# Heads of Q and K in 20 rows each of the DRAM scratch, read back by overlapping loads of 32 rows, one head group a load

## The chip, the cores and the metric

The kernel runs on one core of a Trainium2 chip. A core has TensorE (PE, with its weight loads shown as PEld), VectorE (DVE), ScalarE (ACT), GpSimd (POOL) and SyncE (SP), each with its own stream of instructions, and sixteen DMA engines that carry the transfers which SP and ACT issue. The metric is the device time of one execution in microseconds.

## The reference

The input x has 2048 rows of 640. After a layer norm, two branches are added to x: sliding-window attention with 32 heads of 20 and a window of 256, and a gated MLP with 1536 hidden columns.

```
xn  = layernorm(x)
qkv = xn @ wqkv;  q, k, v: 32 heads x 2048 x 20
p   = softmax(q k^T / sqrt(20)), key j seen by query i when 0 <= i - j < 256
A   = (p v) @ wo
B   = (sigmoid(xn @ w_gate) * (xn @ w_up)) @ w_down
out = x + A + B
```

## The kernel before, in words

The rows go in four chunks of 512 (`CW`). For a chunk, five projection blocks give Q and five give K, each 128 output columns by 512 rows, transposed: output columns on the partitions (`proj_block`, matmuls at L311). DVE copies a Q block to SBUF (L315), ACT a K block (L317), into `st`, of which there are six buffers. SP then stores the block to a DRAM scratch, `sq` or `sk` (L319). The weight columns are picked so that block m holds rows 4m to 4m+3 of every head.

[...] `spread` (L329) loads 128 scratch rows, which are four heads, onto 128 partitions; one load takes two such head groups, 256 KB. There are eight head groups of four heads (`NG` = 8), in two halves of four (`GH`), each half in one `qT` or `kT` tile. The matmul of the scores (L502, in `scores`) reads partitions 32i to 32i+19 of the tile, 20 of the 32.

One pair of scratch tensors serves all chunks, so the stores of the next chunk follow the loads of this one.

Everything that PE does stands in an order written out by hand. `scores` steps (four per pair of head groups in the first chunk, five in the later ones) alternate with pieces of other work that the class `Fill` hands out: gate and up matmuls (`g_gu`, L425 and L432), the next chunk's Q, K and V projections (`g_qk`, `g_v`), and the output products (`g_out`, L446 and L453). PE takes them strictly in that order. ACT takes the exponential of each step's scores (L508), POOL masks it (L519), and `pv` multiplies by V (L535).

The norm of the next chunk is also in there (`g_norms`): DVE normalizes four blocks of rows, SP writes each to a DRAM tile `xs` (L287), reads it back regrouped (L293), and DVE turns it in 32x32 squares into `xnT` (L296), five turns a chunk. The next chunk's projections read `xnT`.

All loads and stores but a few at the very end are issued by SP, in program order. An issue that must wait for a tile, a buffer or an earlier transfer holds back those behind it. Transfers signal on eight semaphores that are used in turn. In SP's queue of the first chunk, the order after the projections is: loads of Q groups 0 and 1, K groups 0 and 1, Q 2 and 3, K 2 and 3; four weight loads of 480 KB (`load_rest`, L180); Q and K groups 4 to 7; the four `xs` writes and four regrouped reads; x rows for chunk 2; eight copies that reorder `wo` in DRAM (`turn_wo`, L207, tile `wo_i`, outermost dimension 4); the loads of `wd`. In a later chunk, the four loads for Q and K of the first half and then the four of the second half follow one another.

Of the kernel before, what the change touches and what calls it, by code (L numbers as in the profile page):

```python
# [9 lines left out]
P = 128  # L10
S = 2048
D = 640
H = 32
DH = 20
# [3 lines left out]
CW = 512  # L18
NCH = S // CW
SBC = CW // P  # L20
HG = 4
NG = H // HG
GH = NG // 2
# [14 lines left out]
BF16 = mybir.dt.bfloat16  # L38
# [55 lines left out]
def kernel(  # L94
# [11 lines left out]
    nc = tc.nc  # L106
# [4 lines left out]
    def pool(name, bufs, **kw):  # L111
        return ctx.enter_context(tc.tile_pool(name=name, bufs=bufs, **kw))

    const = pool("const", 1)
# [5 lines left out]
    kp = pool("kp", 5)  # L120
# [47 lines left out]
    load_wqkv(0)  # L168
    load_wqkv(1)

    scratch = {w: tc.dram_tile([H * 32, CW], BF16, name="s" + w) for w in "qk"}
    zero = kp.tile([P, GH, CW], BF16, name="kT")
    nc.gpsimd.memset(zero[:, 0:3, :], 0.0)

    def clear(w):
        rows = scratch[w].rearrange("(h j) s -> h (j s)", j=32)[:, DH * CW:]
        nc.sync.dma_start(out=rows.rearrange("h (a e) -> h a e", a=4), in_=zero[:, 0:3, :])

    def load_gu(t, w, k, lo=0, hi=FS):
        nc.sync.dma_start(out=t[k][:, :, lo:hi],  # L180
# [2 lines left out]
    load_gu(wg, B_w_gate, 0, 0, FS // 2)  # L183
    load_gu(wu, B_w_up, 0, 0, FS // 2)
    clear("q")
    clear("k")
    load_gu(wg, B_w_gate, 0, FS // 2)

    def load_rest():
        load_gu(wg, B_w_gate, 1, 0, FS // 2)  # L190
        load_gu(wu, B_w_up, 1, 0, FS // 2)
        load_gu(wg, B_w_gate, 1, FS // 2)
        load_gu(wu, B_w_up, 1, FS // 2)
        spread("q", 0, 4, NG)
        spread("k", 0, 4, NG)
# [107 lines left out]
    qk = {}  # L303
    vt = {}

    def proj_block(w, c, m):

        ps = ps_d.tile([P, CW], FP32, name="pqk", tag="d")
        for d in range(DC):
            wt = wqkv["qk".index(w)][:, d, :].rearrange("p (k m) -> p m k", m=DC)  # L310
            nc.tensor.matmul(ps, lhsT=wt[:, m, :], rhs=xnT[c][:, d, :],  # L311
                             start=(d == 0), stop=(d == DC - 1))
        st = stp.tile([P, CW], BF16, name="st")
        if w == "q":
            nc.vector.tensor_copy(out=st, in_=ps)  # L315
        else:
            nc.scalar.copy(out=st, in_=ps)  # L317
        dst = scratch[w].rearrange("(h j) s -> h j s", j=32)
        nc.sync.dma_start(out=dst[:, 4 * m:4 * m + 4, :], in_=st)  # L319

    def spread(w, c, g0, g1):

        half, first = divmod(g0, GH)
        if first == 0:
            qk[w, c, half] = (qp if w == "q" else kp).tile([P, GH, CW], BF16, name=w + "T")
        src = scratch[w].rearrange("(a b p) s -> b p a s", a=2, p=P)
        for b in range(g0 // 2, g1 // 2):
            o = 2 * b - half * GH
            nc.sync.dma_start(out=qk[w, c, half][:, o:o + 2, :], in_=src[b])  # L329

    def new_v(c, s):
        v = vp.tile([P, 2, VH], BF16, name="v")
# [47 lines left out]
    def g_qk(c):  # L380
        for w in "qk":
            for m in range(DC):
                proj_block(w, c, m)
                if c == 0 and w == "q" and m == 1:
                    load_x(1)
                if c == 0 and w == "q" and m == 3:
                    load_gu(wu, B_w_up, 0, FS // 2)
                if c == 1 and w == "q" and m == 3:
                    load_wo()
                if c and w == "k" and m == DC - 1:  # L390
                    spread("q", c, 0, GH)
                yield 5 * MM
        if c == 0:
            spread("q", c, 0, 2)
            spread("k", c, 0, 2)
            spread("q", c, 2, 4)
            spread("k", c, 2, 4)
# [63 lines left out]
    def new_rows(c, s, rows=None, queue=nc.sync):  # L461
        if rows is None:
            rows = lnp.tile([P, D], BF16, name="rows", bufs=3)
        queue.dma_start(out=rows, in_=xr[:, c * SBC + s, :])
        return rows
# [292 lines left out]
    c = NCH - 1  # L758
# [5 lines left out]
    rows = [new_rows(c, s, queue=nc.scalar) for s in range(SBC - 1)]  # L764
# [57 lines left out]
```

## Time and profile before

| | |
|---|---|
| median of three runs | 309.14 us (308.84 to 310.28) |
| the profiled execution | 309.41 us, span 307.7 us, granted PE clock 1.00 |
| PE, ACT, DVE, POOL busy | 98%, 64%, 58%, 55% of the span |
| transfers | 36.87 MB, 120 GB/s over the span |
| SP's issues of Q and K loads | 16 + 16, 256 KB each |
| SP's issues of Q and K stores | 20 + 20, 128 KB each |

The span runs from the first to the last instruction; the profiled execution's own time is 1.71 us longer. An engine's share is its busy time over the span. The page's timeline in 40 slices has 7.7 us to a slice, and its DMA row is the mean busy share of the sixteen DMA engines. In timelines, a line has the start, the duration, the engine, the source line, the operation and its tiles; SPq stands for SP's issuing. An issue's duration is the time in which SP handled it and not that of the transfer. The trace also records when a transfer's parts arrive, one record for each DMA engine that took part.

### The profile page before, as it was taken

What the parts mean: (1) busy time and instruction counts of PE and PEld (TensorE: products, weight loads), DVE (VectorE), ACT (ScalarE), POOL (GpSimd) and SP (SyncE); (2) the same over time, 40 slices, a digit from 0 to 9 for tenths busy, and PEclk for the clock granted to TensorE, in tenths of its full rate; (3) what the DMA queues carried; (4) which work ended last, traced back from release to release, by engine and by line L of the source; (5) the groups of instructions that cost most, each with busy time, mean ns of one, the idle gap of its engine ahead of it and who ended that gap; (6) DMA issues with size and microseconds to landing.
All of it is one profiled execution on the core that took longest, in us unless ns stands there. A gap on an engine that the chain in (4) does not pass through costs nothing.

```text
span 307.7 us, 9969 instructions
## 1 busy us (share of the span) xinstructions
PE 300.1 (98%) x4276; PEld 167.6 (54%) x4311; DVE 178.1 (58%) x355; ACT 198.4 (64%) x197; POOL 168.3 (55%) x307
## 2 busy tenths in 40 slices
PE   7999999999999999999999999999999999999995
PEld 2654444545657654554557664554546664444774
DVE  4735539888675564497946464383734536373423
ACT  5933777698854649888674647878585547678000
POOL 3110687687982928676682728557372937566000
PEclk9999999999999999999999999999999999999999
DMA  7997967886528052800036212730000210000202
GB/s 201 362 336 249 314 201 188 306 244 203 170 92 171 21 179 69 278 33 2 3 131 130 66 58 88 249 123 0 2 2 2 79 34 21 2 2 3 86 21 68
DMA packets 40173, 36.87 MB, mean 120 GB/s; under 512 B 8992, under 2 KB 39840, under 8 KB 40096
## 3 DMA queue, kind: packets, MB, share of 16 engines
q1 hardware_dynamic: 39264, 35.45, 37.7%
q10 hardware_dynamic: 864, 0.77, 0.8%
q8 instruction: 34, 0.56, 0.7%
q14 instruction: 11, 0.09, 0.1%
HBM read 25.59 MB, written 11.44 MB: 120 GB/s over the span
## 4 chain that ended last, share of the span: by engine, by line
PE 96%; DMA 1%; issue 1%; ACT 1%; DVE 0%; SPq 0%
PE y L446 18%; PE pu L432 17%; PE pg L425 17%; PE pqk L311 14%; PE ps L502 9%; PE pv L340 7%; PE y L453 7%; PE acc L535 6%; DMA xc<-in_A_x_dram 1%; PE pt L275 0%; ACT xn L632 0%; ACT xn L637 0%; DVE xn L643 0%; SPq L156 0%; ACT rstd L638 0%
## 5 line engine op out<-in xcount | busy, mean ns | idle before, releaser
L519 POOL TENSOR_SCALAR_AFFINE_SELECT pT<-pT 64x512 bf16<-64x512 bf16 (+1 forms) x256 | 157.1, 614 | 83.3 <-ACT pT L508 71.0
L508 ACT ACTIVATE pT<-ps 128x2048 bf16<-128x2048 f32 (+1 forms) x76 | 141.0, 1855 | 59.7 <-PE ps L502 56.3
L436 DVE SCALAR_TENSOR_TENSOR h<-th,pu 128x512 bf16<-128x512 f32 x48 | 32.7, 680 | 49.7 <-PE pu L432 44.2
L432 PE MATMUL pu<-xnT,wu 128*128 128x512 bf16 x228 | 59.0, 380 | 0.7 <-issue 0.2
L425 PE MATMUL pg<-xnT,wg 128*128 128x512 bf16 x226 | 58.5, 380 | 0.9 <-issue 0.3
L446 PE MATMUL y<-wd,h 128*128 128x320 bf16 (+2 forms) x396 | 56.6, 295 | 0.0
L446 PEld LDWEIGHTS <-h 128*128 128x128 bf16 x396 | 36.8, 98 | 15.6 <-issue 1.8
L428 ACT ACTIVATE th<-pg 128x512 f32<-128x512 f32 x48 | 28.6, 595 | 15.5 <-PE pg L425 15.4
L425 PEld LDWEIGHTS <-wg 128*128 128x128 bf16 x240 | 22.2, 98 | 25.8 <-issue 2.0
L432 PEld LDWEIGHTS <-wu 128*128 128x128 bf16 x240 | 22.0, 98 | 25.5 <-issue 2.0
L502 PE MATMUL ps<-qT,kT 20*64 20x320 bf16 (+4 forms) x1440 | 32.1, 260 | 0.0
L547 DVE STREAM_TRANSPOSE t<-acc 128x512 f32<-128x512 f32 x32 | 21.1, 696 | 16.8 <-PE acc L535 16.8
L502 PEld LDWEIGHTS <-kT 20*64 20x64 bf16 x1440 | 15.4, 103 | 24.8 <-issue 22.2
L457 DVE SCALAR_TENSOR_TENSOR rows<-y,rows 128x320 bf16<-128x320 f32 x30 | 14.5, 488 | 22.5 <-PE y L453 22.4
L559 DVE TENSOR_TENSOR on<-t,rec 128x320 bf16<-128x320 f32 (+4 forms) x48 | 26.4, 551 | 1.1
L340 PE MATMUL pv<-wv,xnT 128*128 128x320 bf16 x160 | 25.9, 300 | 0.0
L453 PE MATMUL y<-wo,oc 128*128 128x320 bf16 (+2 forms) x165 | 24.2, 295 | 0.0
L311 PE MATMUL pqk<-xnT,wk 128*128 128x512 bf16 x97 | 23.1, 381 | 0.2
L311 PE MATMUL pqk<-xnT,wq 128*128 128x512 bf16 x94 | 22.8, 381 | 0.4 <-issue 0.2
L349 DVE CAST v<-pv 64x320 bf16<-64x320 f32 x29 | 14.1, 486 | 11.9 <-PE pv L340 11.6
L535 PE MATMUL acc<-pT,v 64*32 64x320 bf16 (+4 forms) x1440 | 19.6, 253 | 0.0
L535 PEld LDWEIGHTS <-v 64*32 64x32 bf16 x1440 | 16.2, 91 | 5.8 <-issue 1.6
(51 smaller groups left out, 188.1 us busy)
## 6 DMA issues: line engine op xcount, KB each, us to landing
qT<-sq SPq DMA_DIRECT2D x16, 256.0 KB
kT<-sk SPq DMA_DIRECT2D x16, 256.0 KB
sq<-st SPq DMA_DIRECT2D x20, 128.0 KB
sk<-st SPq DMA_DIRECT2D x20, 128.0 KB
out_dram<-rows SPq DMA_DIRECT2D x15, 160.0 KB
wg<-in_B_w_gate_dram SPq DMA_DIRECT2D x4, 480.0 KB
wu<-in_B_w_up_dram SPq DMA_DIRECT2D x4, 480.0 KB
xc<-in_A_x_dram SPq DMA_DIRECT2D x3, 640.0 KB
```

What stands on the lines that cost most here:

```text
L311: nc.tensor.matmul(ps, lhsT=wt[:, m, :], rhs=xnT[c][:, d, :], start=(d == 0), stop=(d == DC - 1))
L340: nc.tensor.matmul(ps[:, 0:HALF], lhsT=xnT[c][:, d, s * P:(s + 1) * P], rhs=wqkv[2][:, d, hf * HALF:(hf + 1) * HALF], start=(d == 0), stop ...
L425: nc.tensor.matmul(pg, lhsT=part(wg, d, f), rhs=xnT[c][:, d, :], start=(d == 0), stop=(d == DC - 1))
L428: nc.scalar.activation(out=th, in_=pg, func=TANH, scale=0.5)
L432: nc.tensor.matmul(pu, lhsT=part(wu, d, f), rhs=xnT[c][:, d, :], start=(d == 0), stop=(d == DC - 1))
L436: nc.vector.scalar_tensor_tensor(out=h, in0=th, scalar=1.0, in1=pu, op0=ADD, op1=MULT)
L446: nc.tensor.matmul(y[:, 0:cut[1] - cut[0]], lhsT=ht[c, f][:, s * P:(s + 1) * P], rhs=wd[:, f, cut[0]:cut[1]], start=(f == 0), stop=False)
L453: nc.tensor.matmul(y[:, 0:cut[1] - cut[0]], lhsT=oc[c, m][:, s * P:(s + 1) * P], rhs=wo[:, m, cut[0]:cut[1]], start=False, stop=(m == DC - 1))
L502: nc.tensor.matmul(ps[a * U:(a + 1) * U, i, col * U:(col + n) * U], lhsT=qk["k", kc, o // GH][32 * i:32 * i + DH, o % GH + a, kb * U:(kb + ...
L508: nc.scalar.activation(out=pt[:, :, 0:width], in_=ps[:, :, 0:width], func=EXP, scale=SCALE)
L519: nc.gpsimd.affine_select(out=view, in_=view, pattern=[[0, HG], [0, n], [sign, U]], compare_op=GE, fill=0.0, base=base, channel_multiplier ...
L535: nc.tensor.matmul(acc[32 * i:32 * i + 32, q * U:(q + n) * U], lhsT=vt[kb][a * U:(a + 1) * U, u, h * VW:h * VW + 32], rhs=pt[a * U:(a + 1) ...
```

## The change

The scratch has 20 rows a head, with 12 rows at the end (`TAIL`) so that the last head can also be read as 32 rows. A load now takes one head group: four heads, 20 rows apart in the scratch, of which 32 rows each are read, so that the 12 rows behind a head's 20 are the first rows of the next head, or the tail. They land on the partitions that the scores do not read. Only the tail is cleared, from a tile of its own of 12x512. The stores have the new stride. There are 64 loads of 128 KB in place of 32 of 256 KB. The matmuls, the scores' operands and the order of work on PE, ACT and DVE stay as they are; after the change the later lines of the kernel are numbered 2 higher.

```
-    scratch = {w: tc.dram_tile([H * 32, CW], BF16, name="s" + w) for w in "qk"}
-    zero = kp.tile([P, GH, CW], BF16, name="kT")
-    nc.gpsimd.memset(zero[:, 0:3, :], 0.0)
+    TAIL = 32 - DH
+    scratch = {w: tc.dram_tile([H * DH + TAIL, CW], BF16, name="s" + w) for w in "qk"}
+    zero = const.tile([TAIL, CW], BF16, name="zero")
+    nc.gpsimd.memset(zero, 0.0)
 
     def clear(w):
-        rows = scratch[w].rearrange("(h j) s -> h (j s)", j=32)[:, DH * CW:]
-        nc.sync.dma_start(out=rows.rearrange("h (a e) -> h a e", a=4), in_=zero[:, 0:3, :])
+        nc.sync.dma_start(out=scratch[w][H * DH:, :], in_=zero)
...
-        dst = scratch[w].rearrange("(h j) s -> h j s", j=32)
+        dst = scratch[w][0:H * DH, :].rearrange("(h j) s -> h j s", j=DH)
         nc.sync.dma_start(out=dst[:, 4 * m:4 * m + 4, :], in_=st)
...
-        src = scratch[w].rearrange("(a b p) s -> b p a s", a=2, p=P)
-        for b in range(g0 // 2, g1 // 2):
-            o = 2 * b - half * GH
-            nc.sync.dma_start(out=qk[w, c, half][:, o:o + 2, :], in_=src[b])
+        rows = scratch[w]
+        for g in range(g0, g1):
+            b, a = divmod(g, 2)
+            src = bass.AP(tensor=rows.tensor, offset=rows.offset + (16 * a + HG * b) * DH * CW,
+                          ap=[[DH * CW, HG], [CW, 32], [1, CW]])
+            nc.sync.dma_start(out=qk[w, c, half][:, g % GH, :], in_=src)
```

## The prediction

> **What bounds the kernel now.** I read the page's table of engines first, then the chain that ended last, then the waits, then the timelines of SP, PE and DVE around the first use of the loaded Q and K, and last a table of stretches.
>
> ```profile
> PE 300.1 (98%) x4276; PEld 167.6 (54%) x4311; DVE 178.1 (58%) x355; ACT 198.4 (64%) x197; POOL 168.3 (55%) x307
> ...
> DMA  7997967886528052800036212730000210000202
> ...
> PE 96%; DMA 1%; issue 1%; ACT 1%; DVE 0%; SPq 0%
> ...
> qT<-sq SPq DMA_DIRECT2D x16, 256.0 KB
> kT<-sk SPq DMA_DIRECT2D x16, 256.0 KB
> ...
> wo_i<-in_A_wo_dram SPq DMA_DIRECT2D x8, 100.0 KB
> ```
>
> TensorE is busy 98% of the span and 96% of the last chain. So no saving of transfers can give more than the few tenths that PE waits, while every transfer that arrives late is paid in full: PE takes its matmuls in written order. The DMA row is at 7 to 9 tenths until about 70 us (slices of 7.7 us): that is where lateness can arise.
>
> From the timelines (start, duration, instruction) of SP, PE and DVE:
>
> ```profile
> 25.55 0.48 SPq L329 DMA_DIRECT2D qT<-sq  x1
> 27.23 0.36 SPq L329 DMA_DIRECT2D kT<-sk  x1
> ...
> 30.64 0.42 PE L502 MATMUL ps<-qT,kT 20*64 20x320 bf16 x16
> ...
> 36.86 3.31 SPq L287 DMA_DIRECT2D xs<-xn  x4
> 44.22 2.45 SPq L293 DMA_DIRECT2D xn<-xs  x4
> ...
> 51.50 1.29 DVE L296 STREAM_TRANSPOSE xnT<-xn 128x512 bf16<-128x512 bf16 x2
> ...
> 54.97 2.35 PE L311 MATMUL pqk<-xnT,wq 128*128 128x512 bf16 x10
> ...
> 78.46 0.43 PE L502 MATMUL ps<-qT,kT 20*64 20x320 bf16 x24
> ```
>
> Three deadlines stand here. The first scores (30.64) need the loads issued at 25.55 and 27.23; the trace records the K load's last arrival at 29.79, so 0.85 us are left. The second chunk's projections (54.97) need the rows that are written to xs, read back regrouped and transposed by DVE; the last regrouped read arrives at 50.19, and DVE turns it from 51.50: 1.3 us left. The second chunk's scores (78.46) need K that arrives at 76.56: 1.9 us left. In chunks 2 and 3 the first loads arrive over 14 us ahead of use.
>
> Busy time and DMA share by stretch (the last three columns are granted clock, DMA share, GB/s):
>
> ```profile
> 52.20:54.00 1.80, 1.64 (x23) 0.79 (x9) 1.80 (x4) 1.45 (x1) 1.01 (x3) 1.00 0.25 85
> ...
> 74.00:80.30 6.30, 6.25 (x74) 3.42 (x73) 4.61 (x11) 6.11 (x8) 5.73 (x14) 1.00 1.01 319
> ```
>
> In the first stretch only the eight copies of wo_i are in flight. Their outermost dimension has 4 entries, and the share is 0.25: four of sixteen DMA engines work. The trace records four arrivals and one early count for each of these copies, against sixteen arrivals for each qT load; and the first wd load behind them has twelve arrivals by 57.57 and four only from 60.79 on. So a copy whose outermost dimension is 4 went through four engines, and what is issued behind it waits there in order. In the second stretch the present qT and kT loads (outermost dimension 128 on both sides) keep all sixteen busy.
>
> **The change part by part.** The profiled execution took 309.41 us: the span 307.7 and 1.71 around it. It lies 0.27 above the median of 309.14. I add to 309.41 and take 0.27 off at the end.
>
> Clears and memset. The memset of 128x1536 takes 1.38 us on POOL and shrinks to about the 0.2 of the ident memset; the POOL results behind it come some 1.2 us earlier. Its reader that waited is the scratch activation on ACT (0.73 us), followed by a wait for the x rows, so nothing on the chain moves: 0. The two clears of 384 KB (SP issue 1.98 and 0.59 us) become 12 KB each. 768 KB at 319 GB/s are 2.4 us of the rings, between 10 and 17 us, when PE works on V and Q projections and waits for DVE and not for a DMA. Cover gone, the gain would be the store latency there (5.3 us against 2.04 for an idle store), but the last K store, which sets the first K load, already took only 2.33. I take 0, bounds 0 and -0.3.
>
> Stores. Same 128 KB, same 32x4x512 shape, another stride: 0. The L502 matmuls read 20 of 32 rows as before: 0.
>
> Loads. The 32 loads of 256 KB become 64 of 128 KB, the same bytes in the same places of SP's order. SP issues 64 x 0.52 (the stores' row) in place of 32 x 0.47: 18 us more over a queue that mostly waits; each in-line 0.5 us is less than the transfer before it takes, so the rings decide. The source pattern is now 4 heads x 32 rows x 512; the destination still 128 partitions. No row of before has 4 on one side and 128 on the other. The bounds are four engines (wo_i, 4 on both sides) and sixteen (the present loads). I take four, since the same factor 4 now leads the source, and only a split into equal parts on both sides serves both patterns.
>
> [...]
>
> Price of one load on four engines. In chunk 1 the last six 256 KB loads arrive from 76.56 to 80.30, 0.75 us apart, sixteen packets of 1 KB an engine. 32 packets an engine take 1.50 us. (wo_i arrivals, 25 KB an engine, are 1.03 apart: 1.31 for 32 KB is the low bound; 319 GB/s gives 1.64, the high one.) Ahead of that stands the fixed part: the first qT load took 2.65 from issue to arrival, less 0.75 is 1.90.
>
> (A) First scores. The first Q load is issued at 25.55 and arrives at 25.55 + 1.90 + 1.50 = 28.95. The same four rings then hold Q group 1, K groups 0 and 1: 30.45, 31.95, 33.45. The step needs all four. PE stands at 30.64, so it stalls 2.8 us (2.1 to 3.4).
>
> (B) Second chunk's projections. Behind these come four more loads (39.45), four weight loads of 480 KB (arrivals now at 35.14, 36.64, 38.14, 39.59: 1.48 apart, so 45.4) and eight loads of groups 4 to 7 (57.4). The four xs writes are queued behind: now 42.55 to 44.17, 1.6 after the last K load, so 59.0. SP cannot be faster, since the regrouped reads (44.22) wait for the last xs arrival (44.17). From there to the last regrouped arrival is 6.0 (50.19): 65.0. DVE then has five turns of 0.67 and one h of 0.64 among them, 4.0: 69.0. The first projection block uses the turned slices one by one and ends about 0.25 later, 69.25, where it now ends at 54.97 + 1.08 = 56.05. PE is 13.2 late, of which A has paid 2.8: 10.4 us (8 to 13, by 1.31 and 1.64 a load). Behind the waiting turns on DVE stand the h products and Q copies; PE waits for both, inside the same stall.
>
> (C) Second chunk's scores. The first Q load there arrives at 74.40 and would at 75.15; the second group of K is the sixth load: 75.15 + 5 x 1.50 = 82.65. Needed at 78.5: 4.1 us (3.2 to 5). Lateness of PE moves both ends.
>
> (D) PE's clock after the stall in B. The ten warming matmuls at the start run 0.43 us apart, a running chain 0.216. A restart as slow for as long as those 4.4 us would cost up to 2.2, mostly inside the stretch that DVE paces: I take 0, bound 2.
>
> What is late next: the second regrouping. In chunk 1 sixteen loads end at 75.15 + 15 x 1.50 = 97.65, or 93.5 on a PE clock shifted by C; xs then 95, regrouped 101, turned 105. Its projections start at 109.38: covered by 4 us, so 0.
>
> Sum: 309.41 + 2.8 + 10.4 + 4.1 - 0.27 = 326.4 us.
>
> **The rivals.** (1) The destination's 128 partitions alone spread each load on sixteen engines. For it: the present loads do so with the same destination. Against: wo_i. Each load is then 0.37 us; K group 1, issued at 27.23 + 0.36 + 0.16, arrives at 27.75 + 1.90 + 0.37 = 30.0, inside the 0.85 us of cover: 309.1, not slower. It decides as soon as a load takes under (30.64 - 25.55 - 1.90) / 4 = 0.80 us.
>
> (2) Four engines, but later transfers overtake on the rings, so that xs and its reads keep their times. For it: nothing but that arrivals within a load spread over 1 to 2 us. Against: the four late arrivals of wd behind wo_i. Only A and C are left: 309.1 + 6.9 = 316.0.
>
> (3) Four engines, and more is late: store buffers (six of stp) held by stores behind wo_i and wd stop ACT's copies and with them the exponentials, the restart is slow (D), and the second regrouping loses its 4 us. For it: four-engine wo_i copies come right behind B in SP's order. Against: covers above. 326.4 + 2 + 2 + 4 = 334.4.
>
> **How the numbers follow.** Forecast 0.72, rival 1 0.12, rival 2 0.08, rival 3 0.08. The forecast's own range is 321 to 332, from the bounds of a load. The range that leaves 2 in 10 out takes in rival 2 and reaches towards rival 3: 315.5 to 334. A change under 0.5% (1.5 us) can't be told from none. Slower holds the forecast and rivals 2 and 3: 0.87 with a little taken off; rival 1 is the same, 0.11; faster, 0.02, would need the early clears to gate something that the waits do not show.
>
> **What would show it.** Four-engine loads: a DMA share near 0.25 while only new loads run, and about 1.5 us between arrivals. A: the first L504 scores start near 33 and wait for a DMA. B: regrouped reads issued near 59 in place of 44, then a PE gap of 7 us or more ahead of pqk. C: a second wait of scores for a DMA, some 13 us later than 78. Past that the distance between the two kernels stays as it is. Scores that start at 30.6 and a share near 1 would make the prediction wrong by rival 1.

## The result and the profile after

The changed kernel takes 330.63 us (median of six runs, 328.65 to 331.48) against 309.71 us (308.84 to 311.19) for the kernel before, a ratio of 1.066 (95% interval 1.061 to 1.071): 6.6% slower. The runs of both kernels come in two groups some 2 us apart: in the profiled execution of the kernel after, a slow clock at the start costs 1.9 us (the last point on the prediction), while what parts the runs of the kernel before stays open. The profiled execution took 331.09 us, with a span of 329.1 and a granted PE clock of 0.973.

From the page of the kernel after, in the order of the page: the table of engines, the granted clock and the DMA share in 40 slices (now of 8.2 us), and the chain that ended last:

```profile
PE 310.0 (94%) x4311; PEld 169.7 (52%) x4311; DVE 178.2 (54%) x355; ACT 198.6 (60%) x197; POOL 166.8 (51%) x307
...
PEclk9899999959997999999999999999999999999999
DMA  7964664577622571522213611232300111000201
...
PE 82%; DMA 10%; DVE 3%; SPq 1%; issue 1%; ACT 1%; DVEq 0%; ACTq 0%
```

DMA holds 10% of the last chain where it held 1%, and PE is busy for 94% of the span in place of 98%. The DMA row lies lower than before in the third to the ninth slice (6466457 against 9796788), although the loads carry as many bytes and the transfers take longer to come: four of sixteen engines work on each (four arrivals a load, and the shares of 0.28 and 0.27 below). The clock row has its two deepest dips in the ninth slice (65.8 to 74.0 us) and the thirteenth (98.7 to 107.0), and a small one in the second.

The same places of the timelines of SP, PE and DVE as before (start, duration, instruction, count; in brackets the idle time ahead of it and what ended it):

```profile
27.40 1.23 SPq L331 DMA_DIRECT2D qT<-sq  x2
28.84 1.05 SPq L331 DMA_DIRECT2D kT<-sk  x2
...
34.31 0.33 PE L504 MATMUL ps<-qT,kT 20*64 20x320 bf16 x4 [1.70 <-DMA kT<-sk]
35.70 0.41 PE L504 MATMUL ps<-qT,kT 20*64 20x320 bf16 x12 [1.06 <-DMA kT<-sk]
...
51.83 3.75 SPq L287 DMA_DIRECT2D xs<-xn  x4
61.24 2.24 SPq L293 DMA_DIRECT2D xn<-xs  x4
...
66.92 1.30 DVE L296 STREAM_TRANSPOSE xnT<-xn 128x512 bf16<-128x512 bf16 x2 [10.09 <-DMA xn<-xs]
...
67.68 1.18 PE L311 MATMUL pqk<-xnT,wq 128*128 128x512 bf16 x2 [7.39 <-DVE xnT L296]
...
97.06 0.33 PE L504 MATMUL ps<-qT,kT 20*64 20x320 bf16 x4 [1.50 <-DMA kT<-sk]
98.45 0.41 PE L504 MATMUL ps<-qT,kT 20*64 20x320 bf16 x20 [1.06 <-DMA kT<-sk]
```

All three deadlines are missed. The first scores wait twice, once for each of two K loads, 1.39 us apart; so do the second chunk's scores. The regrouped reads are issued at 61.24 where they were at 44.22, DVE waits 10.09 us for them, and PE 7.39 for DVE.

Stretches of the kernel after (length; busy time of PE, PEld, DVE, ACT and POOL; granted clock; DMA share; GB/s):

```profile
28.00:34.50 6.50, 4.80 (x26) 1.99 (x24) 5.73 (x15) 1.19 (x2) 0.52 (x2) 1.00 0.28 94
65.40:75.60 10.20, 7.29 (x106) 2.71 (x105) 6.10 (x10) 0.00 (x0) 0.00 (x0) 0.50 0.81 266
93.00:100.00 7.00, 4.44 (x47) 2.34 (x46) 2.45 (x6) 4.27 (x5) 5.53 (x15) 0.97 0.27 96
```

In the first and the third stretch hardly anything but the new loads is in flight, and the share is 0.28 and 0.27: four of sixteen engines. The trace records four arrivals and one early count for every load, as it did for wo_i, and the first four of them (Q groups 0 and 1, then K groups 0 and 1) land at 31.49, 32.89, 34.27 and 35.66. The middle stretch is PE's restart after the long gap: the granted clock is 0.50 for 10.2 us.

Where the time went was read by pairing the 4311 weight loads of PE in both traces and following how much later each one starts:

| place | lateness after it, us | added, us |
|---|---|---|
| start, before any load of Q or K | 1.9 | 1.9 |
| first scores (A) | 5.05 | 3.2 |
| second chunk's first projections (B) | 15.4 | 10.3 |
| clock at 0.50 behind B (D) | 16.9 | 1.5 |
| second chunk's first scores (C) | 19.97 | 3.1 |
| clock at 0.50 behind C | 21.66 | 1.7 |
| all that follows | 21.7 | 0 |

The sum, 21.7, is the difference of the two profiled executions (331.09 - 309.41 = 21.68). The bounds between the rows are good to some 0.4 us: by the end of the first projection block PE is 15.0 us late, and if B ended there, it would be 9.9 and the slow clock behind it 1.9.

### The profile page after: what moved, and what is told of

The parts are those of the page before. It is cut to its first block, busy times and chain, and to the rows that moved or that the text cites. A ratio compares the mean times of both kernels' runs of the same rounds, so it can differ in the third digit from the quotient of the medians.

```text
span 329.1 us, 10036 instructions
## 1 busy us (share of the span) xinstructions
PE 310.0 (94%) x4311; PEld 169.7 (52%) x4311; DVE 178.2 (54%) x355; ACT 198.6 (60%) x197; POOL 166.8 (51%) x307
## 4 chain that ended last, share of the span: by engine, by line
PE 82%; DMA 10%; DVE 3%; SPq 1%; issue 1%; ACT 1%; DVEq 0%; ACTq 0%
PE y L448 16%; PE pu L434 14%; PE pg L427 14%; PE pqk L311 12%; PE ps L504 7%; PE y L455 7%; PE pv L342 6%; PE acc L537 6%; DMA kT<-sk 4%; DMA xs<-xn 2%; DMA wv<-in_A_wqkv_dram 2%; DMA sk<-st 2%; DMA xn<-xs 1%; DVE on L561 1%; DVE st L315 1%
## 5 line engine op out<-in xcount | busy, mean ns | idle before, releaser
L434 PE MATMUL pu<-xnT,wu 128*128 128x512 bf16 x240 | 60.9, 385 | 0.0
L427 PE MATMUL pg<-xnT,wg 128*128 128x512 bf16 x240 | 59.8, 380 | 0.0
L504 PE MATMUL ps<-qT,kT 20*64 20x320 bf16 (+4 forms) x1440 | 33.0, 262 | 5.3 <-DMA kT<-sk 5.3
L311 PE MATMUL pqk<-xnT,wq 128*128 128x512 bf16 x100 | 26.0, 404 | 8.0 <-DVE xnT L296 8.0
L342 PE MATMUL pv<-wv,xnT 128*128 128x320 bf16 x160 | 27.8, 316 | 0.6 <-DMA wv<-in_A_wqkv_dram 0.6
L311 PEld LDWEIGHTS <-wq 128*128 128x128 bf16 x100 | 11.4, 120 | 19.3 <-issue 11.5
L537 PE MATMUL acc<-pT,v 64*32 64x320 bf16 (+4 forms) x1440 | 20.6, 259 | 0.0
```

Of the source, the lines that this page charges most:

```text
L342: nc.tensor.matmul(ps[:, 0:HALF], lhsT=xnT[c][:, d, s * P:(s + 1) * P], rhs=wqkv[2][:, d, hf * HALF:(hf + 1) * HALF], start=(d == 0), stop ...
L427: nc.tensor.matmul(pg, lhsT=part(wg, d, f), rhs=xnT[c][:, d, :], start=(d == 0), stop=(d == DC - 1))
L434: nc.tensor.matmul(pu, lhsT=part(wu, d, f), rhs=xnT[c][:, d, :], start=(d == 0), stop=(d == DC - 1))
L504: nc.tensor.matmul(ps[a * U:(a + 1) * U, i, col * U:(col + n) * U], lhsT=qk["k", kc, o // GH][32 * i:32 * i + DH, o % GH + a, kb * U:(kb + ...
L537: nc.tensor.matmul(acc[32 * i:32 * i + 32, q * U:(q + n) * U], lhsT=vt[kb][a * U:(a + 1) * U, u, h * VW:h * VW + 32], rhs=pt[a * U:(a + 1) ...
```

## The experiments

Three theories were to be told apart. The first, the forecast's, says that a load whose source leads with 4 is served by four engines, and that what stands behind it comes late. The second says that twice as many, smaller loads are the cost. The third says that reading the same scratch rows twice, the overlap, is. Each experiment below was timed beside the kernel before on the same chip, whose medians there were 308.88 (first four), 308.78 (the next three) and 309.03 us (the last two). Unless another kernel is named, the diffs are against the kernel after.

### The same 20-row scratch, with 32 on the outside of both patterns

A load takes 32 rows of one head, for two head groups, so that both source and destination lead with 32. The order of bytes in SP's queue is almost the same; there are 128 loads of 64 KB.

```
-        for g in range(g0, g1):
-            b, a = divmod(g, 2)
-            src = bass.AP(..., ap=[[DH * CW, HG], [CW, 32], [1, CW]])
-            nc.sync.dma_start(out=qk[w, c, half][:, g % GH, :], in_=src)
+        for b in range(g0 // 2, g1 // 2):
+            o = 2 * b - half * GH
+            for i in range(HG):
+                src = bass.AP(tensor=rows.tensor, offset=rows.offset + (HG * b + i) * DH * CW,
+                              ap=[[CW, 32], [16 * DH * CW, 2], [1, CW]])
+                nc.sync.dma_start(out=qk[w, c, half][32 * i:32 * i + 32, o:o + 2, :], in_=src)
```

> Only the loads are changed against the changed kernel: one load takes the 32 rows of one head for two groups (pattern 32 x 2 x 512 on both sides), 128 loads of 64 KB; scratch, overlap and bytes as in the changed kernel. Theory (the engine count follows the 4 that leads the source pattern): sixteen arrivals a load, scores and xnT nearly in time; what is left is SP's doubled issuing, about 1 us at the first scores and 1 to 3 us ahead of the second chunk's projections: 311 to 314 us. Rival 'overlapping reads of the same DRAM rows are slow': stays near 330. Rival 'more loads cost SP too much time': slower than 330, about 345.

It took 317.89 us (317.69 to 319.83), a ratio of 1.031 (1.027 to 1.034). The loads have sixteen arrivals each, and PE reaches the first scores with no wait and at the time of before. From its timelines of PE and SP:

```profile
30.66 0.62 PE L505 MATMUL ps<-qT,kT 20*64 20x320 bf16 x16
...
35.38 8.61 SPq L332 DMA_DIRECT2D qT<-sq  x8
44.03 4.70 SPq L332 DMA_DIRECT2D kT<-sk  x8
49.25 1.88 SPq L287 DMA_DIRECT2D xs<-xn  x4
...
59.41 0.38 PE L311 MATMUL pqk<-xnT,wq 128*128 128x512 bf16 x1 [4.15 <-DVE xnT L296]
```

A is gone with the four engines, and so is C (no wait at the second chunk's scores). But 16 issues of groups 4 to 7, where the kernel before has four, take SP from 35.38 to 48.7, so it comes to the xs writes at 49.25 instead of 36.86; PE's gap of 4.15 us there, with the clock at 0.50 from 59.84 to 66.67 behind it, makes PE 8.5 us late, nearly all of the 9.0 that the kernel loses. The expected size was too small: 1 to 3 us had been put for SP's issuing ahead of the second chunk's projections. An issue of 64 KB that waits for nothing takes SP 0.43 us, but two of these sixteen stand still for 1.2 and 1.9 us, until weight loads issued eight transfers earlier, on the same one of the eight semaphores, have landed (41.48 and 43.67); in the kernel before, the four issues at this place have loads of Q and K eight transfers ahead of them. So this run shows that sixteen engines remove A and C, and that the queue has a price of its own.

### One head group a load, in the kernel before

Here the kernel before, with its 32 rows a head (20 of data and 12 that are cleared once), is split into 64 loads of 128 KB; the source still leads with 128.

```
-        for b in range(g0 // 2, g1 // 2):
-            o = 2 * b - half * GH
-            nc.sync.dma_start(out=qk[w, c, half][:, o:o + 2, :], in_=src[b])
+        for g in range(g0, g1):
+            b, a = divmod(g, 2)
+            nc.sync.dma_start(out=qk[w, c, half][:, g % GH, :], in_=src[b][:, a, :])
```

> The kernel before with one head group a load: 64 loads of 128 KB from 128 contiguous rows of the 32-row scratch. Theory: sixteen engines a load, the extra issues are hidden: 309 to 310.5 us. Rival 'more loads': about 330. Rival 'overlap': 309.

It took 309.75 us (308.70 to 311.87, ten runs, all granted a clock of 0.998 or more), a ratio of 1.003 (1.001 to 1.005), within the half per cent that the prediction counts as no change. Each load has sixteen arrivals. SP's timeline of this kernel:

```profile
25.32 0.85 SPq L329 DMA_DIRECT2D qT<-sq  x2
26.96 0.80 SPq L329 DMA_DIRECT2D kT<-sk  x2
```

Two issues take 0.80 to 0.85 us, or 0.4 each; one of 256 KB took 0.36 to 0.48. The number and size of the loads are not the cause; the second theory falls.

### 33 rows a head: the outer 4 without any overlap

The kernel before with a scratch of 33 rows a head, of which 32 are read and 12 of these cleared as before. No row is read twice and no head's rows are closer than before, but the source can't be written as 128 rows at one distance and leads with 4.

```
+    scratch = {w: tc.dram_tile([H * 33, CW], BF16, name="s" + w) for w in "qk"}
...
+            src = bass.AP(tensor=rows.tensor, offset=rows.offset + (16 * a + HG * b) * 33 * CW,
+                          ap=[[33 * CW, HG], [CW, 32], [1, CW]])
+            nc.sync.dma_start(out=qk[w, c, half][:, g % GH, :], in_=src)
```

> The kernel before with 33 scratch rows a head and one group a load, so the source pattern is 4 x 32 x 512 without any row read twice; 12 rows a head are cleared as before. Theory: four arrivals and one early count a load, and the time of the changed kernel, 329 to 332 us. Rival 'overlap': 309 to 311. Rival 'more loads': 330 too (the run before this one tells that apart).

It took 330.02 us (329.68 to 330.13), a ratio of 1.068 (1.067 to 1.070), as slow as the kernel after. Its timeline of PE at the first scores:

```profile
31.87 0.33 PE L504 MATMUL ps<-qT,kT 20*64 20x320 bf16 x4 [1.53 <-DMA kT<-sk]
33.24 0.64 PE L504 MATMUL ps<-qT,kT 20*64 20x320 bf16 x12 [1.05 <-DMA kT<-sk]
```

And two of its stretches:

```profile
26.00:32.00 6.00, 4.47 (x25) 1.86 (x22) 5.72 (x15) 1.19 (x2) 0.29 (x2) 1.00 0.26 85
33.30:36.60 3.30, 3.25 (x18) 1.16 (x20) 0.00 (x0) 2.31 (x2) 0.67 (x1) 0.50 0.75 187
```

The waits are those of the kernel after, the share is 0.26, and the loads have four arrivals. The overlap is not needed for the loss, and neither are 20-row heads; the third theory falls. The second stretch shows one thing that the kernel after does not have: here the clock fell to 0.50 after the short wait of A too.

### Two heads a load

If the outermost count sets the engines, a load of two heads should have two.

```
-            src = bass.AP(..., ap=[[DH * CW, HG], [CW, 32], [1, CW]])
-            nc.sync.dma_start(out=qk[w, c, half][:, g % GH, :], in_=src)
+            for i in (0, 2):
+                src = bass.AP(..., offset=rows.offset + (16 * a + HG * b + i) * DH * CW,
+                              ap=[[DH * CW, 2], [CW, 32], [1, CW]])
+                nc.sync.dma_start(out=qk[w, c, half][32 * i:32 * i + 64, g % GH, :], in_=src)
```

> The changed kernel with two heads a load (2 x 32 x 512 onto 64 partitions), 128 loads of 64 KB. Theory: two arrivals a load and one early count, 1.4 to 1.5 us a load as before but twice as many of them in a row: about 24 us more ahead of the second chunk's projections, 8 us at each of the two first scores, 365 to 390 us. Rival 'any pattern that cannot be merged runs on four engines' or 'overlap': 330 to 336.

It took 383.24 us (one run), with two arrivals a load, 1.39 us between loads of half the bytes, and this stretch of loads alone:

```profile
30.00:36.00 6.00, 0.67 (x4) 0.10 (x2) 1.95 (x6) 0.00 (x0) 1.27 (x2) 0.94 0.14 48
```

The share is 0.14, two of sixteen being 0.125, and the rate half that of four engines (48 GB/s against 94). So outermost dimensions of 4 and 128 took four engines (share 0.28, four arrivals), 2 and 64 two (0.14, two arrivals), and 32 and 32 sixteen (sixteen arrivals, in the first experiment). Before the prediction only equal sides had been measured; the first two of these pairs are mixed. What other pairs would take was not shown.

### Which part of the loss hangs on which loads

Two kernels use sixteen engines (the loads of the first experiment) for a part of the loads only. In the first, only the first chunk's groups 4 to 7, which stand in SP's queue ahead of the xs writes, are of that kind:

```
+        if c == 0 and g0 >= GH:
+            ... 32 rows of one head for two groups, as above
+        else:
             ... four heads a load, as in the kernel after
```

> The changed kernel with only the loads of groups 4 to 7 of the first chunk done as one head by two groups (16 loads of 64 KB on sixteen engines); all other loads four heads a load. Theory (xs waits behind these loads on the four engines): the xs writes arrive near 53 in place of 61.2, the regrouped reads are issued 7 to 8 us earlier, and PE's gap ahead of the second chunk's projections shrinks from 7.4 us to 0 to 2 us, with it the slow clock behind it: 319 to 323 us. Rival 'SP's order or DVE holds the projections back, not the four engines': 329 to 332.

It took 325.43 us (324.47 to 325.99), a ratio of 1.053 (1.051 to 1.056), 2.4 us over the top of the expected range. SP's timeline, and PE's at the projections:

```profile
51.16 3.02 SPq L287 DMA_DIRECT2D xs<-xn  x4
55.80 1.91 SPq L293 DMA_DIRECT2D xn<-xs  x4
...
62.46 0.38 PE L311 MATMUL pqk<-xnT,wq 128*128 128x512 bf16 x1 [1.50 <-DVE xnT L296]
```

The xs writes are issued no earlier than in the kernel after (51.16 against 51.83), but they land at 54.56 to 55.75 and the regrouped reads go at 55.80 in place of 61.24 (1.9 us of this difference is the late start of the kernel after). In the kernel after, 12 of the sixteen arrivals of each xs write were recorded between 54.32 and 57.02 us and the other four only from 58.56 on, the last of each write at 60.01 to 61.19. The records don't name the engine, but the four late parts of the first write (58.56, 59.25, 59.43, 60.01) come 0.40 us behind the four parts of the last load (58.16, 58.85, 59.03, 59.61), one for one. So the four engines that carry the loads held back four parts of every write, until the last part was 4 to 6 us behind the twelfth: that is B. Together with the slow clock behind it, it adds 5.8 us here and 11.8 in the kernel after. Two things made the expectation miss. The clock falls behind the shorter wait too (0.50 from 63.35 to 70.18), and at the first scores there is a stretch that the kernel after does not have:

```profile
32.60:39.50 6.90, 5.90 (x28) 1.98 (x27) 0.48 (x1) 2.47 (x2) 2.62 (x5) 0.51 0.70 188
```

The clock was at 0.51 for 6.8 us behind A's waits, which cost 2.5 us.

In the second kernel, only the second chunk's loads are of the sixteen-engine kind (`if c == 1`).

> The changed kernel with only the second chunk's loads done as one head by two groups. Theory: the two waits of the second chunk's first scores (1.50 and 1.06 us in the trace of the changed kernel) and the slow clock behind them (1.7 us) go, the rest stays: 325 to 327 us. Rival 'that lateness is inherited from the first chunk and not from these loads': 329 to 332.

It took 325.48 us (324.13 to 326.12), a ratio of 1.053 (1.050 to 1.056). PE's timeline shows the second chunk's first scores without a wait:

```profile
93.38 0.43 PE L513 MATMUL ps<-qT,kT 20*64 20x320 bf16 x24
```

The lateness stays at 15.0 us from there to the end, and the clock does not fall after it. So C, and the fall of the clock behind C, hang on the second chunk's loads.

### What the slow clock behind B is worth

Thirty matmuls on constants, which nothing reads, run ahead of the second chunk's projections, so that PE is busy while it would wait in B.

```
+    def warm(n):
+        ps = ps_d.tile([P, CW], FP32, name="pwarm", tag="d")
+        for k in range(n):
+            nc.tensor.matmul(ps, lhsT=ones[:, 0:P], rhs=ones, start=(k == 0), stop=(k == n - 1))
+        yield 0
+    fill.add("warm", warm(30), 0)
```

> The changed kernel with 30 matmuls of 128x512 on constants put ahead of the second chunk's projections, 6.5 us of work inside the 7.4 us in which PE waits. Theory: the granted clock stays at 1.0 through 65 to 76 us, and the kernel is 1.5 to 3 us faster in spite of the added work: 327 to 329.5 us against 328.7 to 331.5. Rival 'the clock does not fall because of the wait' or 'the slow stretch is hidden behind DVE': no gain, or 1 us slower.

It took 328.91 us (328.43 to 329.46), a ratio of 1.065 (1.063 to 1.067) against 1.066 for the kernel after. The time lies in the expected range, but the ratio shows no gain: the two executions of the kernel after with the highest granted clock (0.979) took 328.65 and 328.82. The clock did stay up. Its stretches, in the same place as those of the kernel after:

```profile
65.40:75.60 10.20, 8.10 (x138) 3.95 (x137) 9.00 (x15) 2.54 (x2) 1.23 (x2) 1.00 0.73 251
```

And PE's timeline at the warming matmuls and at the second chunk's scores:

```profile
59.03 6.74 PE L714 MATMUL pwarm<-const-bfloat16-1.0 128*128 128x512 bf16 x30
...
95.21 0.33 PE L504 MATMUL ps<-qT,kT 20*64 20x320 bf16 x4 [2.84 <-DMA kT<-sk]
96.60 0.41 PE L504 MATMUL ps<-qT,kT 20*64 20x320 bf16 x20 [1.06 <-DMA kT<-sk]
```

PE got ahead by 1.5 us at 72 us, and the next wait for K grew from 1.50 to 2.84 us, which gives nearly all of it back. The second chunk's loads did not start earlier: the first of them is issued at 85.65 here and at 87.47 in the kernel after, whose start was 1.9 us late. In SP's order they stand behind wo_i, wd and the stores. So as long as C is there, the slow clock behind B costs nothing at the end.

### The loads of groups 4 to 7 behind the regrouped reads

In both kernels here, the first chunk's loads of groups 4 to 7 leave `load_rest` and are issued after the regrouped reads of the second chunk's rows (`regroup`, in `g_norms`).

```
 def load_rest():
...
-        spread("q", 0, 4, NG)
-        spread("k", 0, 4, NG)
...
         regroup(c)
+        if c == 1:
+            for g in (4, 6):
+                spread("q", 0, g, g + 2)
+                spread("k", 0, g, g + 2)
```

First with the sixteen-engine loads of the first experiment:

> The kernel with one head by two groups a load everywhere (sixteen engines, 128 loads), and in addition the first chunk's loads of groups 4 to 7 issued behind the regrouped reads of the second chunk in place of ahead of the xs writes. Theory: what remained there was SP's place of the xs writes alone (issued at 49.25 in place of 36.86); with that gone the 20-row scratch costs nothing: 308.5 to 310.5 us. Rival 'the 20-row layout or the doubled issues cost something of their own': 313 to 318.

It took 318.50 us (317.96 to 319.82), a ratio of 1.031 (1.029 to 1.034), no better than without the move. Up to 68.7 us PE stands where it stood before the change, with the xs writes issued at 35.24 to 39.67. Then the waits show a new pair (total, times, longest):

```profile
ACT st L315 <- DMA sq<-st: 9.7, 1, 9.7
PE acc L540 <- ACT st L315: 7.5, 1, 7.5
```

SP now comes to the second chunk's stores behind the moved loads, wo_i and wd, so that all six `st` buffers are taken, the copy of the next block waits for one, and PE's next product waits for that copy. The first four of these stores are issued at 66.26 to 69.47; twelve parts of each have landed by 71.55, and the last four come at 74.99 to 76.27. The first load of wd behind wo_i showed the same split in the kernel before: twelve parts by 57.57, four from 60.79. With the clock at 0.50 from 70.81 to 81.05 as well, PE is 9.8 us late from there on.

The same move with the four-engine loads of the kernel after:

> The changed kernel (four heads a load) with only that same move of the first chunk's loads of groups 4 to 7. Theory: the xs writes no longer stand behind these eight loads, so the gap of 7.4 us ahead of the second chunk's projections goes nearly whole, but the eight loads take 11 us on the four engines behind the regrouped reads, so scores of groups 4 and 5 wait 1 to 2 us, and the waits of 2.8 us at the first and 2.6 us at the second chunk's first scores stay: 317 to 323 us. Rival 'order alone repairs it': 309 to 312. Rival 'order does not matter, the four engines are too slow in total': 328 to 332.

It took 330.80 us (329.72 to 331.05), a ratio of 1.070 (1.067 to 1.072). The gap of B is gone, and in its place stands the same pair, longer, with the clock at 0.50 from 75.59 to 85.83 behind it:

```profile
ACT st L315 <- DMA sq<-st: 11.3, 1, 11.3
PE acc L539 <- ACT st L315: 9.0, 1, 9.0
```

Both expectations failed in the same way: they took the wait away at one place and did not ask what the moved loads would now stand ahead of. The time of the second lies in the range of the rival that gave the order no weight, but the reason given there is not the one that the waits show. Whether more `st` buffers would free this order was not tried. No kernel here was faster than the kernel before.

## Why the prediction was right

**The likeliest case came.** It said 326.4 us, with slower at 0.87, and the median is 330.63, inside the range (315.5 to 334) and inside the likeliest case's own (321 to 332). It is 4.2 us over the number.

**Loads: four engines taken.** Shown, by the share and arrivals of the kernel after, by 33 rows a head without overlap (four arrivals, as slow), by two heads a load (two arrivals), and by 32 rows of one head (sixteen arrivals, no A, no C). The reason given for four, equal parts on both sides, was the author's inference: the runs show the counts, and none shows how they come about. Rival 1, sixteen engines through the destination alone, is out. The price of a load, taken at 1.50 us from bounds of 1.31 and 1.64, measured 1.39 to 1.40: inside, nearer to the wo_i row than to the one that was taken.

**(A) 2.8 us; measured 3.2.** The first load took 4.09 us from issue to arrival (27.40 to 31.49) where 1.90 + 1.50 were put, 0.7 more, and the three behind it came at a price of 1.40 and not 1.50, 0.3 less. Together 2.8 + 0.7 - 0.3 = 3.2.

**(B) 10.4 us; measured 10.3.** The last xs write was put at 59.0 and came at 61.19, of which 1.9 is the late start; the last regrouped read at 65.0 and came at 66.79. The reason given, that writes queue behind the loads on the same engines, is shown by the twelve arrivals on time and the four late ones, and by the halving of B, with the slow clock behind it, when those loads alone change (11.8 to 5.8). That also excludes rival 2, by which the xs writes would overtake. The chain on the page of the kernel after puts 2% on the xs writes, 1% on the regrouped reads and 4% on the K loads.

**(C) 4.1 us; measured 3.1.** The waits were there and hang on the second chunk's loads. Two sizes were off. The price of a load takes 0.5 off (five at 0.1). And the first Q load was put at 75.15, 4.71 us after its issue at 70.44, but it came 3.95 us after its issue (87.47 to 91.42), no later than before the change (70.44 to 74.40), which takes off 0.8: 2.8 are left. The prediction let lateness move both ends alike. Here it did, but by luck: PE and the issue of the loads were both 17.0 us late, PE only because of the slow clock behind B. With the warming matmuls PE was 13.8 us late and the loads 15.2, and C came to 4.3.

**(D) The clock, taken as 0 with a bound of 2.** This term was mis-sized. The clock was at 0.50 for 10.24 us behind B, where the ten warming matmuls had suggested 4.4, and cost 1.5 us at that place; behind C's wait it was at 0.50 again, from 99.53 to 102.94, for another 1.7. The first of the two is not the loss that it seems: with the clock kept up, C takes it back. The second is a net loss that goes away with C. So D and C together, forecast at 4.1, came to 1.5 + 3.1 + 1.7 = 6.3.

**Next late: the second regrouping, taken as 0.** Right: its last read comes at 121.51, and PE has no gap there. The distance between the kernels stays at 21.7.

**Clears and memset, stores: 0.** The table shows no gain before A. Neither was tried alone.

**Rival 3, more is late.** Of its three parts the slow restart was real. The store buffers were not the wait in the kernel after, where the projections themselves are late enough; they are what stops PE as soon as the order is changed so that B goes, in both last runs. So its argument was right one step further on.

**What was not foreseen: 1.9 us at the start.** In the profiled execution of the kernel after, the clock was at 0.50 from 7.37 to 10.78 us, behind a wait of 0.59 us for `wv` and ahead of the first load of Q or K; in that of before it was at 1.00 there. The stretch in the kernel after:

```profile
7.37:10.78 3.41, 3.22 (x16) 2.06 (x16) 1.19 (x4) 2.74 (x8) 0.00 (x0) 0.50 1.05 377
```

No trace of an experiment has a fall there, though seven of these kernels start with the same instructions. So it comes with the execution and not with the change. The executions of 328.65 and 328.82 us had a mean granted clock of 0.979 against 0.973 of the profiled one, and 3.41 us at 0.50 are worth 0.005 of it; where in them the clock fell is not on record. Without the start, 19.8 of the 21.7 us between the two profiled executions are left, of which the prediction's sum had 17.3 (2.8 + 10.4 + 4.1); the 2.5 us between are the two falls of the clock (3.2), less the 0.7 by which A, B and C together came out smaller (16.6 against 17.3).

## What to carry to other kernels

Before a transfer is cut into fewer or denser rows, look at the outermost dimension of both sides: here 4 against 128 took four engines of sixteen for the same bytes, and 33 rows a head cost as much as 20. Price such a load twice, once for its own reader and once for every transfer behind it on the same engines: the reader paid 3.2 us, and the xs writes, of which a quarter lay behind the loads, 10.3. And where a stall is taken away by more issues or by another order, ask what then stands behind them in the queue: 32 issues in place of eight ahead of the xs writes brought SP to these 12.4 us later, and the moved loads kept the store buffers full and stopped PE for 7.5 and 9.0 us.

## What was not expected of the hardware

The granted clock fell in pieces of about 3.41 us or whole multiples: 7.37 to 10.78 and 99.53 to 102.94 (3.41), 32.63 to 39.46 in the kernel with sixteen engines for groups 4 to 7 (6.83), 65.40 to 75.64 (10.24). In each of them it was at 0.50. The first record of the full clock stands between 3.91 and 5.96 us in the traces of this case, at 3.96 in the kernel after and at 5.26 in the kernel before. Whether this difference makes some executions 1.9 us slower at the start was not shown: no run here sets the place of that record.

The clock fell behind waits as short as those of A too (1.53 and 1.05 us with 33 rows a head), and the traces show which. Count stretches of 3.41 us from the first record of the full clock on: in all eleven traces every change of the clock falls on an edge of these. Of the 970 stretches at full clock, 23 have 1.74 us or more in which PE is idle, and 22 of them are followed by a fall (the other one, with 1.99 us, is in the kernel with the warming matmuls); of the other 947 one is, with 1.72 us. A fall went on for another stretch where PE was idle for 0.62 us or more of one at 0.50 (28 of 28), and ended where it was idle for 0.34 or less (23 of 23). The waits of A lie within one stretch in the kernel with 33 rows a head (2.56 us idle), where the clock fell, and across two in the kernel after (1.73 and 1.02) and with sixteen engines in the second chunk (1.62 and 1.07), where it did not. Behind B in the kernel after, the three stretches at 0.50 have 2.29, 0.62 and 0.00 us idle. At the start of the kernel after, the stretch ahead of the fall has 1.78, against 0.42 to 1.44 in the other ten traces. This is a pattern read from the traces; no kernel here was built to test it.
